# Turned tiles in the idle accumulator's bank, attention sums in the scores' bank, masks added by TensorE, and one granule kept whole in PSUM

## The chip, the cores and the metric

The kernel runs on one core of one Trainium2 chip. The metric is the device time of one execution in microseconds (us); a time of a kernel is the median of several runs. The profile shows one execution.

## The reference

The input x has 2048 rows of 1024 numbers. Its rows are normalised (layer norm) to xn, and the output is

    out = x + A(xn) + B(xn)

A is a recurrent attention over segments of 32 rows. Eight memory rows are carried from segment to segment:

```
mask[i, k] = (i < 8) or (i >= k)              # 40 x 40, row i asks, row k answers
for s in range(64):
    h = concat(mem, xn[32 s : 32 s + 32])     # 40 rows
    q, k, v = h Wq, h Wk, h Wv                # 32 heads of 128
    p = softmax(where(mask, q k^T / sqrt(128), -1e9))
    o = (p v) Wo                              # 40 rows of 1024
    mem = o[0:8];  out_A[segment s] = o[8:40]
```

B picks the two rows of xn with the highest router score and adds a gated MLP of them (1024 to 3584 and back). It runs at the end and is not touched by the change.

## The kernel before, in words

**Tiles.** A segment has 24 new rows that are computed at once with the eight memory rows (32 rows, `XM` = 24 and the memory), and eight left-over rows (`XL` = 8) that nothing later in the recurrence needs. The left-over rows of four segments are put together into one tile of 32 rows and go through the same weights in "left passes", spread by hand over the four segments of a group (`PASSES`, `COPIES`; j = s mod 4 is the place of a segment in its group). The matmuls have 32 columns of stationary data, so four of them stand side by side in the array (`tile_position`).

**Weights.** The weights are cut into 64 granules of 128 x 2048 bf16 (512 KB): 0 to 47 are Wq, Wk and Wv in six phases of eight (`PHASES`: q0, k0, q1, k1, v0, v1, the digit is the half of the heads), 48 to 63 are Wo. 44 granules stay in SBUF. Twenty (`STREAMED`) are read anew in every segment through a ring of five slots (`wstream`, tile `g`), in order, on SP's queue: whenever a streamed granule has been used (`release`, `after`), `fetch` issues the next of the list. From segment 1 on they come from a copy in DRAM (`wsc`), which segment 0 writes.

**Granules kept in PSUM.** Granule 6 (`KEPT_WHOLE`) lies whole in two PSUM banks and is copied back to SBUF in every segment (`bring_back`), with no transfer. The right half of granule 25 (`KEPT_PART`) lies in a third bank. Its left half (256 KB) is still streamed, and `kept_piece` copies two quarters of 512 columns into its slot on VectorE (hooks (2, 1) and (2, 2)). `keep` writes the kept pieces into PSUM in segment 0, by two transposes.

**PSUM.** There are eight banks of 2 KB per partition: two accumulators (`psA`, tiles PSm, WO), one for left passes (`psL`, PSl and WL), one for scores (`psS`, tile BS), one for turned tiles (`psT`, tile BT, with its parts `PTB`, `PTB2` and `OPB`), three for kept granules (`psK`). BS also holds the rows' means and deviations (`MR`, `ML`).

**One segment.** Phase p runs eight granules into PSm; ScalarE casts it to XB (L793) or VM (L803). Small work is hung on places (p, kc), that is behind granule 8 p + kc, by `hook`; TensorE runs it there in program order. At (p + 1, 3) `transposes` turns XB into BT (L624) and copies it out as QT (L632) or KT (L639). `turn_lx` and `new_qkl` do so for the left-over rows' q and k. `scores` at (2, 6) and (4, 6) writes the products into BS (L647, L649); VectorE then adds the masks there in three instructions (L656, L658), takes the maximum (L661) and subtracts it (L662). `exponent` (ScalarE, L666) and `soften` (VectorE, L671 to L682, the last read of BS is L679) follow at (3, 4) and (5, 0). `attend(half, ph)` multiplies by V (L696, L698) for two of the four column groups, and copies the sums to OT and OTL (L705, L707). It runs at (5, 4) and (5, 6) for half 0, with its sums in WO's bank and in BT, and inside the loop over Wo's granules at w = 5 and w = 8 for half 1, with its sums in BS and BT. With the last one the next segment's rows are turned into BT (`turn_rows`, L293). Wo's products go to WO (`project`, L574); VectorE adds them to x (L842), the memory rows are turned into the next segment's ST (`mem_to_st`), and the next segment starts.

**Order.** Each engine runs its instructions in the order of the program (`manual_schedule`); waits between engines are placed automatically from what each tile's bank holds.

Of the kernel before, what the change touches and what calls it, by code (L numbers as in the profile page):

```python
# [20 lines left out]
KEPT_PART = 25  # L21
# [29 lines left out]
def kernel(  # L51
# [69 lines left out]
    psT = ctx.enter_context(tc.tile_pool(name="psT", bufs=1, space=PSUM))  # L121
# [12 lines left out]
    wsc = {g: dram.tile([P, columns(g, 1).stop - columns(g, 1).start], BF16, name=f"wsc{g}")  # L134
           for g in streamed if g != KEPT_WHOLE}
# [19 lines left out]
    NEGR = CT[:, 13:14]  # L155
# [5 lines left out]
    BT = psT.tile([P, 512], F32, name="BT")  # L161
    SPS = BS[:, 0:8 * NK].rearrange("p (i a k) -> p i a k", i=4, a=2)
    PTB = BT[:, 0:256].bitcast(BF16)
    PTB2 = BT[:, 256:512].bitcast(BF16)
    OPB = BT[:, 256:256 + 4 * NK]
# [58 lines left out]
    def spread(t0, t1):  # L224
# [3 lines left out]
        PD = OPB  # L228
# [22 lines left out]
    def router_out():  # L251
        nc.vector.tensor_copy(out=RB, in_=RF)
        nc.tensor.transpose(out=PTB[0:NT, 0:P], in_=RB, identity=IDENT[:, :])
        RT = home(hx, [NT, P], BF16, "RT")
        nc.vector.tensor_copy(out=RT[:, :], in_=PTB[0:NT, 0:P])
        nc.gpsimd.dma_start(out=r_d[0].rearrange("(t p) -> t p", p=P), in_=RT[:, :])
# [33 lines left out]
    def turn(src, at=0):  # L290
        PTx = PTB[:, 256 * at:256 * (at + 1)].rearrange("p (c g r) -> p c g r", c=2, g=4)
# [12 lines left out]
    def new_st(turned):  # L304
        PTx, PTl = turned
# [23 lines left out]
    def sum_left(t, G):  # L329
# [31 lines left out]
    def keep(g, t):  # L361
        for c, K in KEPT_COLS[g].items():
            turned = PTB.rearrange("p (i r) -> p i r", i=4)
            for i in range(4):
                nc.tensor.transpose(out=turned[:, i, :], in_=t[:, 512 * c + P * i:512 * c + P * (i + 1)],
                                    identity=IDENT[:, :])
            XK = one.tile([P, 512], BF16, tag="vl0", name="XK")
            nc.vector.tensor_copy(out=XK[:, :], in_=PTB)
# [118 lines left out]
    def turn_lx():  # L487
        PTq = PTB2.rearrange("p (i c) -> p i c", i=4)
# [3 lines left out]
    def new_qkl():  # L492
        t = qkl[0] = one.tile([P, 4, 4, 4, XL], BF16, tag="bC", name="QKL")
        nc.scalar.copy(out=t.rearrange("p i m q r -> p (i m q r)"), in_=PTB2)

    def turn_first(mat, half, XBl):
        if mat == 0 and half == 0:
            qkl[0] = one.tile([P, 4, 4, 4, XL], BF16, tag="bC", name="QKL")
        PTq = PTB.rearrange("p (i c) -> p i c", i=4)
        for il in range(4):  # L500
            nc.tensor.transpose(out=PTq[:, il, :], in_=XBl[:, il * P:(il + 1) * P], identity=IDENT[:, :])
        nc.scalar.copy(out=qkl[0][:, :, 2 * half + mat, :, :],  # L502
                       in_=PTB.rearrange("p (i q s r) -> p i q s r", i=4, q=4, s=4)[:, :, :, 0, :])
# [103 lines left out]
    for s in range(NSEG):  # L607
# [7 lines left out]
        QT, KT, PTs, OT, nxt, sums = {}, {}, {}, {}, {}, {}  # L615
# [5 lines left out]
        def transposes(mat, half, XB):  # L621
            PTq = PTB.rearrange("p (i j r) -> p i j r", i=4, j=4)
# [3 lines left out]
            pv = PTq.rearrange("p i j r -> p (i j) r")  # L626
            with_left = s > 0 and mat == 0 and half == 0
# [13 lines left out]
        def scores(half):  # L641
            QKL = qkl[0]
            q, k = QT[half], KT[half]
            for il in range(4):
                for jq in range(4):
                    hh = 4 * il + jq
                    nc.tensor.matmul(SPS[32 * jq:32 * jq + 32, il, 0, :], lhsT=q[:, hh, :], rhs=k[:, hh, :],  # L647
                                     start=(il == 0), stop=True, tile_position=(0, 32 * jq), skip_group_check=True)
# [3 lines left out]
            for S4, m in ((SPS[:, :, 0, 0:XM], MASK), (SPS[:, :, 0, SEG:NK], None),  # L652
                          (SPS[:, :, 1, SEG:NK], MASK[:, 0:XL])):
                if m is not None:
                    m = m.unsqueeze(1).to_broadcast([P, 4, S4.shape[2]])
                    nc.vector.tensor_tensor(out=S4, in0=S4, in1=m, op=ALU.add)  # L656
                else:
                    nc.vector.tensor_scalar(out=S4, in0=S4, scalar1=NEGR, scalar2=None, op0=ALU.add)  # L658
# [26 lines left out]
        def attend(half, ph, turn_too=None):  # L685
            if half not in OT:
# [3 lines left out]
                sums[half] = [BS[:, 0:4 * NK] if half else nxt["wo"][:, 256:256 + 4 * NK], OPB]  # L690
            PTm, PTl = PTs[half]
            for il in range(4):
                for jl in range(2):
                    q0 = 32 * (2 * ph + jl)
                    o = sums[half][jl][:, il * NK:(il + 1) * NK]
# [6 lines left out]
            for jl in range(2):  # L702
                ov = sums[half][jl].rearrange("p (i q) -> p i q", i=4)
                copy = nc.scalar.copy if half == 0 or jl == 0 else nc.vector.tensor_copy
                copy(out=OT[half][:, 2 * ph + jl, :, :], in_=ov[:, :, 0:SEG])  # L705
                h0 = 16 * half + 8 * ph + 4 * jl
                copy(out=left_out()[:, h0:h0 + 4, j, :], in_=ov[:, :, SEG:NK])  # L707


# [53 lines left out]
        hook(5, 4, lambda: attend(0, 0))  # L763
        hook(5, 6, lambda: attend(0, 1))

        for p, (mat, half) in enumerate(PHASES):
# [24 lines left out]
            if mat < 2:  # L791
                XB = one.tile([P, 512], BF16, tag=("bE", "kt")[mat], name="XB")
                nc.scalar.copy(out=XB[:, :], in_=PSm[:, :])  # L793
                hooks.setdefault((p + 1, 3), []).insert(0, lambda m=mat, h=half, b=XB: transposes(m, h, b))
# [6 lines left out]
            else:  # L801
                VM[half] = one.tile([P, 512], BF16, tag=("bC", "bA")[half], name="VM")
                nc.scalar.copy(out=VM[half][:, :], in_=PSm[:, :])  # L803
                while stores:
# [7 lines left out]
        if s + 1 < NSEG:  # L812
            xn = norm_seg(s + 1)
            left_too = nxt["xl"] if j == 0 and G + 1 < NT else None
            turned = []
# [154 lines left out]
```

## Time and profile before

| | |
|---|---|
| time, median of 3 runs | 1903.38 us (1899.34 to 1905.05) |
| the profiled execution | 1896.06 us, span 1894.4 us |
| mean granted TensorE clock | 0.96 of full speed |
| TensorE matmul busy | 1572.3 us, 83% |
| VectorE, ScalarE, GpSimd busy | 875.6, 683.5, 441.5 us |
| moved by DMA | 712.41 MB, mean 376 GB/s |
| segment 0 done | at about 130 us; segments 1 to 63 until 1838 us, then B |

The profiled execution is somewhat quicker than the median of the runs; sums made in the profile are held against its own time. A row of the order of time reads: start, duration, engine, line, operation, tile written <- tiles read, shapes, count, and in brackets the idle time before it with what ended it. Rows of matmuls carry a modelled end, so rows that follow each other overlap. `g` is a slot of the ring, `wres` a resident granule.

### The profile page before, as it was taken

The page shows a single profiled execution, that of the slowest core. Times are in us where ns is not written, and L with a number is a line of the kernel's source. Part 1 is how long each engine was busy: PE and PEld are TensorE (multiplying, and loading weights), DVE is VectorE, ACT ScalarE, POOL GpSimd, SP SyncE. Part 2 cuts the span into 40 slices and gives each one's busy share as a digit, 9 for nine tenths or more (in the row PEclk, how much of TensorE's full clock was granted, in tenths as well). Part 3 has the DMA queues.
Part 4 walks back from the last instruction along what each step waited for, and adds up shares of the span by engine and source line. Part 5 has one row for each costly group of instructions (what it writes and reads, how often), then busy time and mean ns, then how long its engine had stood idle before and what let it go on. Part 6 is the DMA issues. An engine that isn't in the chain of part 4 may idle for free.

```text
span 1894.4 us, 82425 instructions
## 1 busy us (share of the span) xinstructions
PE 1572.3 (83%) x36000; PEld 880.0 (46%) x36000; DVE 875.6 (46%) x2865; ACT 683.5 (36%) x1916; POOL 441.5 (23%) x882
## 2 busy tenths in 40 slices
PE   3458888889888888898888988888888889888864
PEld 1124545455454444445454545445444554545443
DVE  6734544445444444544454444444444454444430
ACT  1123433344333433434333334333433343433320
POOL 3111313213131322213121322213132221312120
PEclk8669999999999999999999999999999999999985
DMA  9999999999999999999999999999999999999998
GB/s 370 398 368 379 369 386 373 391 378 390 393 360 375 368 380 372 379 372 374 401 365 374 370 388 370 355 383 374 379 364 387 377 392 378 364 395 362 374 388 331
DMA packets 232121, 712.41 MB, mean 376 GB/s; under 512 B 39296, under 2 KB 53168, under 8 KB 231760
## 3 DMA queue, kind: packets, MB, share of 16 engines
q1 hardware_dynamic: 194384, 671.18, 92.9%
q0 software_dynamic: 28736, 28.09, 4.6%
q10 hardware_dynamic: 8640, 7.87, 1.2%
q8 instruction: 282, 4.62, 0.9%
q14 instruction: 79, 0.65, 0.1%
HBM read 694.32 MB, written 22.29 MB: 378 GB/s over the span
## 4 chain that ended last, share of the span: by engine, by line
DMA 53%; PE 38%; DVE 5%; issue 2%; ACT 1%; SPq 1%; ACTq 0%; DVEq 0%
DMA g<-wsc 47%; PE PSm L774 21%; PE WO L574 4%; PE PSl L567 4%; PE BT L624 3%; PE WL L574 2%; DMA XP<-in_A_x_dram 2%; DMA MW<-in_B_w_gate_dram 1%; DVE XR L248 1%; DMA MW<-in_B_w_up_dram 1%; DMA g<-in_A_Wq_dram 1%; DMA wres<-in_A_Wo_dram 1%; PE BS L647 1%; DMA g<-in_A_Wo_dram 1%; PE BT L293 1%
## 5 line engine op out<-in xcount | busy, mean ns | idle before, releaser
L774 PE MATMUL PSm<-wres,ST 128*32 128x512 bf16 x8448 | 706.5, 383 | 9.1 <-DMA wres<-in_A_Wv_dram 3.5
L774 PEld LDWEIGHTS <-ST 128*32 128x32 bf16 x12288 | 328.6, 96 | 403.5 <-issue 176.3
L774 PE MATMUL PSm<-g,ST 128*32 128x512 bf16 x3588 | 361.9, 387 | 106.2 <-DMA g<-wsc 81.5
L574 PEld LDWEIGHTS <-OT 128*32 128x32 bf16 x8192 | 219.2, 97 | 153.3 <-issue 135.8
L793 ACT CAST XB<-PSm 128x512 bf16<-128x512 f32 x256 | 150.1, 586 | 310.8 <-PE PSm L774 309.9
L574 PE MATMUL WO<-wres,OT 128*32 128x256 bf16 x5632 | 238.3, 278 | 13.7 <-DMA wres<-in_A_Wo_dram 7.9
L483 POOL DMA_DIRECT2D LX<-ql_d x63 | 33.6, 533 | 825.9 <-PE WO L574 396.5
L574 PE MATMUL WO<-g,OT 128*32 128x256 bf16 x2560 | 132.3, 281 | 83.6 <-DMA g<-wsc 74.1
L567 PE MATMUL PSl<-wres,STL 128*32 128x512 bf16 x2112 | 192.7, 391 | 0.0
L844 POOL DMA_DIRECT2D out_dram<-X x256 | 129.4, 512 | 217.1 <-DVE X L842 168.3
L639 DVE COPY KT<-BT 128x512 bf16<-128x512 bf16 x112 | 45.7, 408 | 283.3 <-ACT XB L793 119.0
L273 POOL DMA_DIRECT2D X<-in_A_x_dram x256 | 129.7, 510 | 186.4 <-PE PSm L774 83.8
L377 ACT COPY BK<-KEPT 128x512 bf16<-128x512 bf16 x126 | 74.4, 590 | 129.3 <-PE WO L574 98.3
L632 ACT COPY QT<-BT 128x512 bf16<-128x512 bf16 x128 | 74.9, 585 | 122.2 <-PE BT L490 70.3
L567 PEld LDWEIGHTS <-STL 128*32 128x32 bf16 x3072 | 83.6, 98 | 54.0 <-issue 8.4
L624 PEld LDWEIGHTS <-XB 128*128 128x128 bf16 x1024 | 58.5, 98 | 107.6 <-ACT XB L793 66.4
L842 DVE TENSOR_TENSOR X<-WO,X 128x256 bf16<-128x256 f32 x64 | 27.2, 424 | 170.9 <-PE WO L574 170.9
L803 ACT CAST VM<-PSm 128x512 bf16<-128x512 f32 x128 | 75.6, 591 | 81.2 <-PE PSm L774 79.6
L696 PEld LDWEIGHTS <-VM 32*128 32x128 bf16 x2048 | 66.1, 91 | 82.9 <-issue 69.9
L624 PE MATMUL BT<-IDENT,XB 128*128 128x128 bf16 x1024 | 102.0, 222 | 1.4 <-ACT QKL L502 1.4
L381 DVE COPY g<-KEPT 128x512 bf16<-128x512 bf16 x126 | 47.6, 419 | 118.2 <-PE PSm L774 74.4
L705 DVE CAST OT<-BT 128x128 bf16<-128x128 f32 x128 | 37.3, 291 | 129.8 <-PE BT L293 68.8
(168 smaller groups left out, 2378.9 us busy)
## 6 DMA issues: line engine op xcount, KB each, us to landing
g<-wsc SPq DMA_DIRECT2D x1134, 512.0 KB, 6.1
g<-wsc SPq DMA_DIRECT2D x63, 256.0 KB, 5.4
LX<-ql_d POOLq DMA_DIRECT2D x63, 128.0 KB, 5.9
ql_d<-XBl ACTq DMA_DIRECT2D x60, 128.0 KB, 5.6
MW<-in_B_w_gate_dram SPq DMA_DIRECT2D x16, 448.0 KB, 9.1
MW<-in_B_w_up_dram SPq DMA_DIRECT2D x16, 448.0 KB, 9.1
wres<-in_A_Wk_dram SPq DMA_DIRECT2D x12, 512.0 KB, 11.5
MW<-in_B_w_down_dram SPq DMA_DIRECT2D x12, 512.0 KB, 10.1
```

Of the source, the lines that this page charges most:

```text
L273: nc.gpsimd.dma_start(out=X[s % 2][32 * g:32 * g + XM, :], in_=x2[s * SEG:s * SEG + XM, 256 * g:256 * (g + 1)])
L377: copy(out=back[c][:, :], in_=KEPT_COLS[KEPT_WHOLE][c])
L381: copy(out=t[:, 512 * c:512 * (c + 1)], in_=KEPT_COLS[g][c])
L567: nc.tensor.matmul(PSl[32 * jq:32 * jq + 32, :], lhsT=STL[:, g % KC, :], rhs=part(Gv, jq), start=first_, stop=last_, tile_position=(0, 32 ...
L574: nc.tensor.matmul(PS[32 * g:32 * g + 32, 0:256], lhsT=lhs(h), rhs=Gv[:, D * hs + 256 * g:D * hs + 256 * (g + 1)], start=(first and hs == ...
L624: nc.tensor.transpose(out=PTq[:, il, :, :].rearrange("p j r -> p (j r)"), in_=XB[:, il * P:(il + 1) * P], identity=IDENT[:, :])
L632: nc.scalar.copy(out=QT[half][:, :, :], in_=pv)
L696: nc.tensor.matmul(o, lhsT=VM[half][q0:q0 + 32, il * P:(il + 1) * P], rhs=PTm[q0:q0 + 32, il, 0:NK], start=True, stop=False, tile_position ...
L774: nc.tensor.matmul(PSm[32 * jq:32 * jq + 32, :], lhsT=ST[:, kc, :], rhs=part(Gv, jq), start=(kc == 0), stop=(kc == KC - 1), tile_position= ...
L793: nc.scalar.copy(out=XB[:, :], in_=PSm[:, :])
L803: nc.scalar.copy(out=VM[half][:, :], in_=PSm[:, :])
L844: nc.gpsimd.dma_start(out=out2[s * SEG:s * SEG + XM, 256 * g:256 * (g + 1)], in_=OB[32 * g:32 * g + XM, :])
```

## The change

Tile BT and its bank go. What lay there lies elsewhere:

- Turned tiles (`turned(n)`, half n of 256 fp32 columns) lie in the accumulator that is idle: `idle[0]` is the last PSm that has been cast out. The next phase but one writes into this bank again.
- The attention sums of half 0 lie in WO's bank (as before) and in BS; those of half 1 in the idle accumulator and in BS. The hooks of `attend(0, ...)` move from (5, 4) and (5, 6) to (5, 5) and (5, 7).
- The masks are no longer added by VectorE behind the scores. TensorE writes them into BS before the scores, in three matmuls with the identity, behind the transposes of k at (2, 3) and (4, 3); the scores accumulate on them. The row constant `NEGR` becomes bf16.
- The freed bank is a fourth one for kept granules: granule 25 (`KEPT_SLOT`) is kept whole. From segment 1 on nothing of it is loaded and nothing of it is written to `wsc`. It still takes its turn in the ring's slots, and four copies fill the slot: the first on ScalarE at (1, 7), three on VectorE at (2, 0), (2, 1) and (2, 2).
- `norm_left` moves from (5, 3) to (4, 4) in segments after the first.

```diff
-KEPT_PART = 25
+KEPT_SLOT = 25
...
-        if s > 0 and g == KEPT_WHOLE:
+        if s > 0 and g in (KEPT_WHOLE, KEPT_SLOT):
             return None
-        return slice(0, 1024 if s > 0 and g == KEPT_PART else 2048)
+        return slice(0, 2048)
...
-    BT = psT.tile([P, 512], F32, name="BT")
+    idle = [psA.tile([P, 512], F32, tag="acc", name="START")]
+
+    def turned(n=0):
+        return idle[0][:, 256 * n:256 * (n + 1)].bitcast(BF16)
...
-    KEPT = [psK.tile([P, 1024], BF16, name=f"KEPT{b}") for b in range(3)]
-    KEPT_COLS = {KEPT_WHOLE: {0: KEPT[0][:, 0:512], 1: KEPT[0][:, 512:1024], 2: KEPT[1][:, 0:512], 3: KEPT[1][:, 512:1024]},
-                 KEPT_PART: {2: KEPT[2][:, 0:512], 3: KEPT[2][:, 512:1024]}}
+    KEPT = [psK.tile([P, 1024], BF16, name=f"KEPT{b}") for b in range(4)]
+    KEPT_COLS = {g: {c: KEPT[2 * n + c // 2][:, 512 * (c % 2):512 * (c % 2 + 1)] for c in range(4)}
+                 for n, g in enumerate((KEPT_WHOLE, KEPT_SLOT))}
...
         def transposes(mat, half, XB):
-            PTq = PTB.rearrange("p (i j r) -> p i j r", i=4, j=4)
+            PTq = turned().rearrange("p (i j r) -> p i j r", i=4, j=4)
...
+            if mat == 1:
+                for S4, m in ((SPS[:, :, 0, 0:XM], MASK), (SPS[:, :, 0, SEG:NK], NEGR.to_broadcast([P, XL])),
+                              (SPS[:, :, 1, SEG:NK], MASK[:, 0:XL])):
+                    nc.tensor.matmul(S4, lhsT=IDENT[:, :], rhs=m.unsqueeze(1).to_broadcast([P, 4, S4.shape[2]]),
+                                     start=(m is MASK), stop=False, skip_group_check=True)
...
                     nc.tensor.matmul(SPS[32 * jq:32 * jq + 32, il, 0, :], lhsT=q[:, hh, :], rhs=k[:, hh, :],
-                                     start=(il == 0), stop=True, tile_position=(0, 32 * jq), skip_group_check=True)
+                                     start=False, stop=True, tile_position=(0, 32 * jq), skip_group_check=True)
...
-            for S4, m in ((SPS[:, :, 0, 0:XM], MASK), (SPS[:, :, 0, SEG:NK], None),
-                          (SPS[:, :, 1, SEG:NK], MASK[:, 0:XL])):
-                if m is not None:
-                    m = m.unsqueeze(1).to_broadcast([P, 4, S4.shape[2]])
-                    nc.vector.tensor_tensor(out=S4, in0=S4, in1=m, op=ALU.add)
-                else:
-                    nc.vector.tensor_scalar(out=S4, in0=S4, scalar1=NEGR, scalar2=None, op0=ALU.add)
...
-        def attend(half, ph, turn_too=None):
+        def attend(half, quads, turn_too=None):
...
-                sums[half] = [BS[:, 0:4 * NK] if half else nxt["wo"][:, 256:256 + 4 * NK], OPB]
+            banks = [(idle[0] if half else nxt["wo"])[:, 256:256 + 4 * NK], BS[:, 0:4 * NK]]
...
-            hook(2, 1, lambda: kept_piece(KEPT_PART, 2, nc.vector.tensor_copy))
-            hook(2, 2, lambda: kept_piece(KEPT_PART, 3, nc.vector.tensor_copy))
+            for c in range(4):
+                hook(1 + (c + 7) // 8, (c + 7) % 8, lambda c=c: kept_piece(KEPT_SLOT, c, (nc.scalar.copy if c == 0 else
+                                                                                         nc.vector.tensor_copy)))
...
-            hook(5, 3, lambda: norm_left(nxt["xl"], G + 1))
+            hook(*((4, 4) if s > 0 else (5, 7)), lambda: norm_left(nxt["xl"], G + 1))
...
-        hook(5, 4, lambda: attend(0, 0))
-        hook(5, 6, lambda: attend(0, 1))
+        hook(5, 5, lambda: attend(0, [0, 1]))
+        hook(5, 7, lambda: attend(0, [2, 3]))
...
                 nc.scalar.copy(out=XB[:, :], in_=PSm[:, :])
+                idle[0] = PSm
```

In the other places PTB and PTB2 become `turned()` and `turned(1)`, and OPB becomes `idle[0]`.

More of the change, by code (lines that the diff above doesn't have):

```diff
@@ L252, in router_out @@
         nc.vector.tensor_copy(out=RB, in_=RF)
-        nc.tensor.transpose(out=PTB[0:NT, 0:P], in_=RB, identity=IDENT[:, :])
+        PTR = turned()[0:NT, 0:P]
+        nc.tensor.transpose(out=PTR, in_=RB, identity=IDENT[:, :])
         RT = home(hx, [NT, P], BF16, "RT")
-        nc.vector.tensor_copy(out=RT[:, :], in_=PTB[0:NT, 0:P])
+        nc.vector.tensor_copy(out=RT[:, :], in_=PTR)
         nc.gpsimd.dma_start(out=r_d[0].rearrange("(t p) -> t p", p=P), in_=RT[:, :])
@@ L493, in new_qkl @@
         t = qkl[0] = one.tile([P, 4, 4, 4, XL], BF16, tag="bC", name="QKL")
-        nc.scalar.copy(out=t.rearrange("p i m q r -> p (i m q r)"), in_=PTB2)
+        nc.scalar.copy(out=t.rearrange("p i m q r -> p (i m q r)"), in_=turned(1))
     def turn_first(mat, half, XBl):
@@ L701, in attend @@
                 turn_too()
[L702 to L706, printed above, removed]
+            for n, (quad, sum_) in enumerate(sums.items()):
+                ov = sum_.rearrange("p (i q) -> p i q", i=4)
+                copy = nc.vector.tensor_copy if n and half else nc.scalar.copy
+                copy(out=OT[half][:, quad, :, :], in_=ov[:, :, 0:SEG])
+                h0 = 16 * half + 4 * quad
                 copy(out=left_out()[:, h0:h0 + 4, j, :], in_=ov[:, :, SEG:NK])
@@ L803 @@
                 nc.scalar.copy(out=VM[half][:, :], in_=PSm[:, :])
+                idle[0] = PSm
                 while stores:
@@ L877 @@
                                 op0=ALU.subtract, op1=ALU.mult)
-    PXS = PTB[:, 0:2 * KC].rearrange("p (k c) -> p k c", c=2)
+    idle[0] = psA.tile([P, 512], F32, tag="acc", name="PXS")
+    PXS = turned()[:, 0:2 * KC].rearrange("p (k c) -> p k c", c=2)
     for kc in range(KC):
```

47 lines of the change are left out of this document (22 added, 25 removed).

## The prediction

> **What bounds the kernel now.** I read the profile page first: the busy shares, the DMA slices, the queues and the chain.
>
> ```profile
> span 1894.4 us, 82425 instructions
> PE 1572.3 (83%) x36000; PEld 880.0 (46%) x36000; DVE 875.6 (46%) x2865; ACT 683.5 (36%) x1916; POOL 441.5 (23%) x882
> ...
> DMA  9999999999999999999999999999999999999998
> ...
> q1 hardware_dynamic: 194384, 671.18, 92.9%
> ...
> DMA 53%; PE 38%; DVE 5%; issue 2%; ACT 1%; SPq 1%; ACTq 0%; DVEq 0%
> ```
>
> TensorE is the busiest engine by the first row, but the DMA row stands at 9 in all slices but the last, and more than half of the ending chain is DMA. So the question is whether TensorE has slack left. Next I asked for the windows: all segments from the second on, then one segment with j = s mod 4 = 2 and the j = 3 segment behind it (columns: length, busy time and count per engine, granted clock, DMA share, GB/s).
>
> ```profile
> 129.40:1837.75 1708.35, 1496.93 (x34690) 838.23 (x34690) 791.99 (x2646) 661.91 (x1866) 406.38 (x805) 0.99 1.00 376
> 1348.91:1375.25 26.34, 22.86 (x525) 12.26 (x520) 12.12 (x40) 10.33 (x29) 4.70 (x10) 1.00 0.99 379
> 1375.25:1403.06 27.81, 25.55 (x601) 14.20 (x597) 12.22 (x40) 11.30 (x31) 6.93 (x14) 1.00 1.00 369
> ```
>
> The DMA share is 1.00 over 63 segments, which take 1708.35 / 63 = 27.1 us each. Then TensorE's order of time in the j = 2 segment and the waits of the whole span.
>
> ```profile
> 1364.69 0.40 PE L774 MATMUL PSm<-g,ST 128*32 128x512 bf16 x4 [0.47 <-DMA g<-wsc]
> 1364.90 0.62 PE L774 MATMUL PSm<-wres,ST 128*32 128x512 bf16 x8
> 1365.91 0.40 PE L774 MATMUL PSm<-g,ST 128*32 128x512 bf16 x4 [0.39 <-DMA g<-wsc]
> ...
> 1374.58 0.40 PE L574 MATMUL WO<-g,OT 128*32 128x256 bf16 x8 [0.41 <-DMA g<-wsc]
> ```
>
> ```profile
> PE PSm L774 <- DMA g<-wsc: 81.5, 173, 1.7
> PE WO L574 <- DMA g<-wsc: 74.1, 161, 1.9
> DVE OT L705 <- PE BT L293: 68.8, 63, 2.7
> PE WO L696 <- ACT OTL L707: 11.5, 15, 2.1
> ```
>
> The rows with `g` are streamed granules 39, 42 and, last, 62. From 39 to 62 there are eight steps in 9.89 us: 1.24 us for each granule of 512 KB. In the second half of a segment TensorE runs at the pace at which granules land. It waited 81.5 + 74.1 = 155.6 us in 334 waits, 2.5 us a segment. More is hidden: a granule's row lasts 0.40 us, yet the next starts 0.21 us behind it (1364.69, 1364.90), and a wait is counted only from the modelled end; 334 times 0.19 us adds 1.0 us a segment. So TensorE's path without these waits is about 27.1 - 3.5 = 23.6 us against 27.1 us of transfers, and the DMA is the bound.
>
> **The change part by part.**
>
> *The transfer removed.* Granule 25's second load goes.
>
> ```profile
> g<-wsc SPq DMA_DIRECT2D x1134, 512.0 KB, 6.1
> g<-wsc SPq DMA_DIRECT2D x63, 256.0 KB, 5.4
> ```
>
> 63 loads of 256 KB leave SP's queue. At 1.24 us for 512 KB one is worth 0.62 us; at the queue's mean (92.9% of 1894.4 us is 1760 us for 671.18 MB, so 0.262 MB take 0.69 us) a little more. Upper end: 63 x 0.69 = 43 us. Segment 0 also no longer writes these 256 KB out, about 1 us.
>
> *Copies instead.* All four quarters of granule 25 now come out of PSUM, two more than before: one on ScalarE at phase 1, one on VectorE at phase 2.
>
> ```profile
> L377 ACT COPY BK<-KEPT 128x512 bf16<-128x512 bf16 x126 | 74.4, 590 | 129.3 <-PE WO L574 98.3 <-issue 31.0
> L381 DVE COPY g<-KEPT 128x512 bf16<-128x512 bf16 x126 | 47.6, 419 | 118.2 <-PE PSm L774 74.4 <-DMA g<-wsc 27.9 <-PE PSl L567 15.9
> L656 DVE TENSOR_TENSOR BS<-BS,CT 128x96 f32<-128x96 f32 (+1 forms) x256 | 59.6, 233 | 80.5 <-PE BS L649 76.0
> L658 DVE TENSOR_SCALAR BS<-BS,CT 128x32 f32<-128x32 f32 x128 | 33.1, 259 | 4.5
> ```
>
> They cost 0.59 and 0.42 us on engines that are 36% and 46% busy, and wait only for a slot freed in phase 0. The DVE copies stand idle before (118.2 us in all), so no one is late: zero, or about 0.3 us on TensorE where the ScalarE copy pushes the next XB. VectorE loses the masks: (59.6 + 33.1) / 63 = 1.5 us a segment.
>
> *Masks on TensorE.* Three identity matmuls per half, six a segment, behind the four transposes.
>
> ```profile
> 1362.42 0.40 PE L624 MATMUL BT<-IDENT,XB 128*128 128x128 bf16 x4
> 1362.75 0.40 PE L774 MATMUL PSm<-g,ST 128*32 128x512 bf16 x4
> ...
> L370 PE MATMUL KEPT<-IDENT,XK 128*128 128x128 bf16 x24 | 3.2, 279 | 11.6 <-DVE XK L368 11.6
> ```
>
> Four identity matmuls of 128 columns take 0.33 us from start to the next start, 0.08 each; the dearest identity group has 0.28. No such masks are in the trace, so 0.08 and 0.28 are the ends; they are nearest to the transposes beside which they stand, and I take 0.09: 0.55 us a segment (ends 0.5 and 1.7). A gain is excluded here, as TensorE had none of this work.
>
> *Attention sums in the scores' bank.* `attend(0, ...)` now writes BS and so must wait until `soften(1)` has read it (L679); before, it could run ahead. Behind it on TensorE stand granules 46, 47 and all of Wo.
>
> ```profile
> 1364.34 0.27 DVE L656 TENSOR_TENSOR BS<-BS,CT 128x96 f32<-128x96 f32 x1 [0.56 <-PE BS L649]
> ...
> 1365.16 0.49 DVE L661 TENSOR_REDUCE NM<-BS 128x8 f32<-128x320 f32 x1
> ...
> 1367.78 0.21 DVE L679 TENSOR_TENSOR OTL<-BS,DN 128x64 bf16<-128x64 f32 x1
> ```
>
> Today BS is free at 1367.99, 3.65 us after the first mask. Without masks the reduce takes the first mask's place, 0.82 us earlier, so 2.83 us remain, and about 3.1 us from the scores' last matmul. TensorE by itself needs seven granules, 7 x 0.215 = 1.5 us, to reach the new hook (5, 5): it would stand 1.4 us in j = 0 and 2. In j = 1 three passes for the left-over rows before that hook (0.65 us) fill half of this, in j = 3 six fill nearly all. Mean 0.9 us (ends 0 and 1.5).
>
> *Banks shared.* The waits row `DVE OT L705 <- PE BT L293` shows that copies out of one part of a bank are ordered behind writes to another part. So Wo's first matmuls wait until ScalarE has copied the sums that lie in WO's bank:
>
> ```profile
> 905.78 0.19 ACT L707 CAST OTL<-WO 128x32 bf16<-128x32 f32 x1
> ```
>
> ```profile
> 905.63 0.40 PE L774 MATMUL PSm<-g,ST 128*32 128x512 bf16 x4
> 906.02 0.62 PE L574 MATMUL WO<-wres,OT 128*32 128x256 bf16 x16
> ```
>
> The copy ends at 905.97, Wo starts at 906.02, 0.39 us behind a granule that lasts 0.215. With the second attend moved behind granule 47 that cover is gone: 0.3 us more. Likewise PSm of phase p + 2 waits for the copies out of the turned tile:
>
> ```profile
> 893.42 0.82 PE L774 MATMUL PSm<-wres,ST 128*32 128x512 bf16 x12
> ```
>
> ```profile
> 893.57 0.59 ACT L494 COPY QKL<-BT 128x512 bf16<-128x512 bf16 x1
> ```
>
> The x12 are granules 14, 15 and 16, so phase 2 begins at 893.85, the copy ends at 894.16: 0.3 us of wait, 0.25 on the mean, since passes fill it in j = 2. In phases 3 to 5 the copies end first.
>
> *Sum.* TensorE gets 0.55 + 0.9 + 0.3 + 0.25 = 2.0 us a segment, 25.6 us in all, and the transfers 27.1 - 0.65 = 26.5 us. The transfers stay the bound by 0.9 us on the mean; with the high ends (1.7 + 1.5 + 0.3 + 0.3 = 3.8) TensorE would, by 0.9.
>
> j = 3 is tighter: in its last third TensorE hardly waits for the DMA. There one wait goes:
>
> ```profile
> 1395.33 0.18 ACT L707 CAST OTL<-WO 128x32 bf16<-128x32 f32 x1 [1.46 <-DVE PT L682]
> ```
>
> `attend(0, 1)` waits 0.8 us there for this copy (the row `PE WO L696 <- ACT OTL L707`: 11.5 us in 15 waits), which hangs on `soften(1)`, 0.82 us earlier without masks. That pays for the masks and Wo's wait; I keep 0.2 us of gain there. Elsewhere I keep 0.6 of 0.65, as the margin varies: 47 x 0.6 + 16 x 0.2 = 31 us, of which I take off 1 us for granule 25's two more pieces in segment 0, where four more transposes and a copy for each lie beside loads. The profiled execution took 1896.06 us (span 1894.4), so 1866; the median of the runs is 1903.38, 7 us above it, so 1873.
>
> **The rivals.**
>
> *TensorE takes half of it back* (0.17). The wait for BS is 1.5 us in every segment, and phase 4 also waits 0.3: 2.9 us on TensorE, level with the transfers at 26.5. Where two limits are level each wins at times; I put it at 12 us of gain, 1891. For it: in j = 0 and 2 there are no passes in phase 5. Against: five slots let TensorE be two granules late, 2.5 us, at no cost.
>
> *The masks make TensorE the bound* (0.14, slower). The mask matmuls write four separate runs of 24 or 8 columns, which no matmul of the trace does. Should each last as long as a 512-column matmul from start to modelled end, 0.40, six cost 2.4 us instead of 0.55, the path is 27.5 us, 0.4 above today's 27.1, and 63 x 0.4 = 25 us are lost: 1928. It decides from 0.34 us a matmul (2.05 us for six). Against: the rows of identity matmuls with contiguous output, 0.08 in step. The Trainium skill, "PSUM — Partial Sum Buffer", Specifications (TRN2), says that any non-contiguous access pattern slows matmuls significantly and gives no figure; no run here shows it yet, and by that rule the time is this rival's.
>
> *Nothing is gained* (0.09). Granule 25's slot carries no transfer from phase 0 to phase 3, so at most four loads are in flight, not five; were the rate set by their number, the queue would lose what it saves: 1903, give or take 4. For it: a load lands 6.1 us after issue, about the time of five. Against: the DMA share is 1.00, so the engines have work throughout, and 256 KB less landed only 0.7 us sooner.
>
> **How the numbers follow.** Forecast 0.60: 1873, its own range 1860 (all 43 us) to 1886. The range 1858 to 1897 takes in the second case and part of the fourth and leaves out the slower one. About 0.3%, 5.7 us, is what a measurement can tell from no change. Faster: 0.60 and nearly all of the second, 0.76; same: most of the fourth, 0.08; slower: the third and the rest of the fourth, 0.16.
>
> **What would show it.** Right: no 256 KB loads from wsc; DMA share 1.00 again; segments of about 26.6 us; the waits of TensorE for `g<-wsc` down from 155.6 us to near 60; new waits of `attend` for VectorE's L679 and of Wo for ScalarE; six mask matmuls in about 0.09 us steps. Wrong: a DMA share under 0.98 in j = 0 to 2, waits for DMA almost gone with segments of 27 us (TensorE the bound), or a granule pitch above 1.3 us in phase 5.

## The result: slower by 1.1%

The changed kernel takes 1922.83 us (median of four runs, 1921.66 to 1924.08) against 1901.74 us (1899.34 to 1905.05): 1.011 times as long, 95% interval 1.009 to 1.0129. Some 31 us were forecast to go; 21 us came.

The page of the profile after, the rows that answer to those of before:

```profile
span 1920.1 us, 82800 instructions
PE 1595.6 (83%) x36400; PEld 913.4 (48%) x36400; DVE 809.5 (42%) x2546; ACT 702.2 (37%) x1979; POOL 442.1 (23%) x881
...
DMA  9999999999999999999999999999999999999998
...
q1 hardware_dynamic: 185312, 654.66, 90.8%
...
DMA 45%; PE 43%; DVE 5%; ACT 4%; issue 3%; SPq 0%; ACTq 0%; POOL 0%; DVEq 0%
...
g<-wsc SPq DMA_DIRECT2D x1134, 512.0 KB, 6.0
```

The 256 KB loads are gone and 16.5 MB less is moved by q1. The slices of the DMA row still stand at 9. A load takes 6.0 us instead of 6.1. The window over the same 63 segments (length, busy time and count by engine, granted clock, DMA share, GB/s):

```profile
129.21:1862.63 1733.42, 1517.32 (x35068) 868.78 (x35068) 726.69 (x2330) 680.89 (x1929) 407.16 (x805) 0.98 0.98 361
```

A segment takes 1733.42 / 63 = 27.51 us, against 27.12. The loss of 0.40 us a segment lies in the recurrence and not in segment 0 or B. The rate fell from 376 to 361 GB/s: fewer bytes were moved, and the time did not fall. TensorE's waits after:

```profile
PE PSm L775 <- DMA g<-wsc: 93.7, 173, 1.7
...
PE WO L576 <- ACT OTL L709: 34.8, 64, 0.9
PE WO L576 <- DMA g<-wsc: 27.4, 61, 1.8
...
PE PSm L775 <- ACT QKL L496: 7.4, 37, 0.2
PE BS L698 <- DVE BX L679: 4.8, 10, 0.9
PE BS L698 <- DVE OTL L679: 3.0, 7, 0.8
```

The waits for loads fell from 155.6 to 121.1 us, those of Wo for loads from 74.1 to 27.4, while those of PSm rose from 81.5 to 93.7. New waits stand in front of Wo: 34.8 us for the copy of the left-over rows' sums out of WO's bank, in 64 waits, one in each segment.

### The profile page after: what moved, and what is told of

Read it like the earlier page. It is cut to its first block, busy times and chain, and to the rows that moved or that the text cites. A ratio compares the mean times of both kernels' runs of the same rounds, so it can differ in the third digit from the quotient of the medians.

```text
span 1920.1 us, 82800 instructions
## 1 busy us (share of the span) xinstructions
PE 1595.6 (83%) x36400; PEld 913.4 (48%) x36400; DVE 809.5 (42%) x2546; ACT 702.2 (37%) x1979; POOL 442.1 (23%) x881
## 4 chain that ended last, share of the span: by engine, by line
DMA 45%; PE 43%; DVE 5%; ACT 4%; issue 3%; SPq 0%; ACTq 0%; POOL 0%; DVEq 0%
DMA g<-wsc 37%; PE PSm L775 20%; PE WO L576 8%; PE PSl L569 4%; PE PSm L626 3%; DMA XP<-in_A_x_dram 2%; PE WL L576 1%; DMA MW<-in_B_w_gate_dram 1%; DMA MW<-in_B_w_up_dram 1%; ACT QKL L496 1%; DVE XR L249 1%; DVE DN L671 1%; ACT VL L593 1%; PE PSm L698 1%; DMA g<-in_A_Wq_dram 1%
## 5 line engine op out<-in xcount | busy, mean ns | idle before, releaser
L775 PE MATMUL PSm<-wres,ST 128*32 128x512 bf16 x8448 | 713.8, 383 | 17.2 <-ACT QKL L496 7.4
L775 PE MATMUL PSm<-g,ST 128*32 128x512 bf16 x3588 | 361.3, 385 | 109.4 <-DMA g<-wsc 93.7
L576 PE MATMUL WO<-wres,OT 128*32 128x256 bf16 x5632 | 246.8, 287 | 45.6 <-ACT OTL L709 34.8
L383 DVE COPY g<-KEPT 128x512 bf16<-128x512 bf16 x189 | 68.5, 418 | 382.4 <-ACT g L383 336.9
L576 PE MATMUL WO<-g,OT 128*32 128x256 bf16 x2560 | 137.1, 287 | 36.0 <-DMA g<-wsc 27.4
L639 ACT COPY QT<-PSm 128x512 bf16<-128x512 bf16 x128 | 74.9, 585 | 130.9 <-PE PSm L492 77.7
L671 DVE TENSOR_REDUCE DN<-BS 128x8 f32<-128x320 f32 x128 | 62.9, 491 | 133.1 <-ACT BS L666 133.1
L698 PE MATMUL BS<-PT,VM 32*128 32x40 bf16 x1024 | 87.7, 178 | 20.3 <-DVE RI L270 9.4
L626 PE MATMUL PSm<-IDENT,XB 128*128 128x128 bf16 x1024 | 102.0, 222 | 1.6 <-ACT QKL L504 1.4
L661 DVE TENSOR_REDUCE NM<-BS 128x8 f32<-128x320 f32 x128 | 62.8, 491 | 77.1 <-PE BS L656 77.1
```

The lines of the kernel that those rows point to most:

```text
L576: nc.tensor.matmul(PS[32 * g:32 * g + 32, 0:256], lhsT=lhs(h), rhs=Gv[:, D * hs + 256 * g:D * hs + 256 * (g + 1)], start=(first and hs == ...
L626: nc.tensor.transpose(out=PTq[:, il, :, :].rearrange("p j r -> p (j r)"), in_=XB[:, il * P:(il + 1) * P], identity=IDENT[:, :])
L639: nc.scalar.copy(out=QT[half][:, :, :], in_=pv)
L671: nc.vector.tensor_reduce(out=DN[:, :], in_=S8, axis=AX.X, op=ALU.add)
L698: nc.tensor.matmul(o, lhsT=VM[half][q0:q0 + 32, il * P:(il + 1) * P], rhs=PTm[q0:q0 + 32, il, 0:NK], start=True, stop=False, tile_position ...
L775: nc.tensor.matmul(PSm[32 * jq:32 * jq + 32, :], lhsT=ST[:, kc, :], rhs=part(Gv, jq), start=(kc == 0), stop=(kc == KC - 1), tile_position= ...
```

## The experiments

Ratios are to the kernel before, run on the same chip, with 95% intervals.

### Structure and transfer apart

**e1_structure_only**: the changed kernel with granule 25 as before (right half kept, left half loaded, two copies).

```diff
-        return slice(0, 2048)
+        return slice(0, 1024 if s > 0 and g == KEPT_SLOT else 2048)
```

> The changed kernel, but granule 25 is loaded by half as before (256 KB a segment come back; the freed bank stays empty). Theory P (pace): from granule 9 to 36 TensorE sets the pace, so the transfer saved there buys nothing, and what the change adds on TensorE costs the 20 us. Then loading the half again costs next to nothing: 1923, 1917 to 1930. Theory S (dead slot): the slot that granule 25 holds without a transfer keeps the queue from running ahead, which itself costs; with the half loaded again it costs as little as before: 1910 to 1917. Theory T (my forecast's prices): the transfer is worth 40 us and the moves cost 60: 1950 to 1965.

Measured: 1915.24 us, 1.0073 (1.0037 to 1.0108). It lies in the range of theory S, though the interval reaches into that of P.

**e2_no_transfer**: the kernel before, with no load of granule 25 and four copies into its slot.

```diff
+            for c in range(4):
+                hook(1 + (c + 7) // 8, (c + 7) % 8, lambda c=c: kept_piece(KEPT_PART, c, (nc.scalar.copy if c == 0 else nc.vector.tensor_copy)))
```

> The kernel before, but nothing of granule 25 is loaded from segment 1 on: its slot is still taken in turn and filled by four copies out of PSUM, at the changed kernel's places (its left half gets the right half's numbers, so this part of the computation is changed). Nothing else moves. P: 1896 to 1903, as the transfer buys nothing there. S: 1900 to 1912, the dead slot costs what the transfer saves, or more. T: 1858 to 1870.

Measured: 1909.69 us, 1.0033 (1.0005 to 1.0061), again in the range of S. So the saved load with its copies is no gain but a small loss by itself, and 0.73% + 0.33% is about the 1.1% of the whole change: the two parts add up.

**e3_out_of_ring**: the kernel before, granule 25 takes no slot; the resident granule 24 is read for it, without copies.

```diff
-                Gv = back if s > 0 and g == KEPT_WHOLE else granule(g)
+                Gv = back if s > 0 and g == KEPT_WHOLE else granule(24 if s > 0 and g == KEPT_PART else g)
```

> The kernel before, but granule 25 is out of the ring from segment 1 on: no transfer, no slot, no copies (the phase reads granule 24 twice, so this part of the computation is changed). P: 1893 to 1903, no better than with the dead slot but for the copies. S: 1858 to 1872, since all five slots carry transfers. T: 1858 to 1870, the same as with the dead slot.

Measured: 1888.3 us, 0.9903 (0.9858 to 0.9948). No range takes it in: P began at 1893, S and T ended at 1872 and 1870.

**e8_dead_slot_one_copy**: as e2, but one copy alone into the slot; three quarters are read from granule 24.

```diff
+                if s > 0 and g == KEPT_PART:
+                    Gv = [res_tiles[24][:, 512 * c:512 * (c + 1)] for c in range(3)] + [Gv[:, 1536:2048]]
```

> The kernel before with granule 25's slot taken and not loaded, as e2, but only one quarter copied out of PSUM; the other three quarters are read from resident granule 24 (this part of the computation is changed). If the dead slot is what parts e2 from e3: 1903 to 1911, as e2. If the four copies are: 1884 to 1892, as e3.

Measured: 1899.67 us, 0.9982 (0.9958 to 1.0006), between the two ranges. Taken one after the other: with load, slot and two copies gone it is -1.0% (e3). With the slot held again and one copy into it, +0.8% (e8 against e3, the intervals lie apart). With three copies more, +0.5% (e2 against e8, the intervals just meet at their ends). While the slot is held, the load and one copy less are worth 0.2% (e8), with an interval that reaches to no gain at all. The forecast had -2.3% at most for the load, none for the slot and about none for the copies.

### The parts of the structure

**e4_attend_back**, **e5_masks_back** and **e6_turned_back** are e1 with one of its parts as before: the attention sums in a bank of their own with the old hooks, the masks on VectorE, the turned tiles in a bank of their own.

```diff
e4: -        hook(5, 5, lambda: attend(0, [0, 1]))
    +        hook(5, 4, lambda: attend(0, [0, 1]))
e5: +                    nc.vector.tensor_tensor(out=S4, in0=S4, in1=m, op=ALU.add)
e6: -        return idle[0][:, 256 * n:256 * (n + 1)].bitcast(BF16)
    +        return BT[:, 256 * n:256 * (n + 1)].bitcast(BF16)
```

> As e1_structure_only (granule 25 loaded by half), and the attention sums lie again in BS, WO and a bank of their own, with attend at (5, 4) and (5, 6). Left of the change: turned tiles in the idle accumulator and masks on TensorE. If the waits of attend for soften and of Wo for ScalarE cost the most (P as I priced it, 1.2 of 2.0 us a segment): 1905 to 1912. If masks and the turned tiles cost it: 1917 to 1923. If attend's waits are hidden by the DMA: as e1.

> As e1_structure_only (+14 us to the kernel before), with the masks added by VectorE again. If the masks' six matmuls are what costs TensorE most: 1900 to 1908, beside 1902 before. If shortening soften's chain matters more to attend, which now waits for it, than the matmuls cost: 1918 to 1935, since BS comes free 0.82 us later in each half. If the two cancel: 1912 to 1918.

> As e1_structure_only, with the turned tiles in a bank of their own again (attention sums and masks stay as changed). If the wait of a phase for the copies out of the idle accumulator (0.25 us a segment by my sum) is all on the path: 1898 to 1904. If it is hidden by the DMA: 1912 to 1919, as e1.

Measured: 1913.42 us, 1.0048 (1.0024 to 1.0073); 1956.49 us, 1.0279 (1.0237 to 1.0322); 1907.04 us, 1.0018 (0.9992 to 1.0043). Against e1's 1.0073 the turned tiles in the accumulator cost about 0.55% and the attention sums in BS about 0.25%. Both intervals overlap e1's, so these two sizes are only indicated; e4 and e6 lie between their ranges. That the masks belong on TensorE, once `attend` waits for `soften`, is clear: on VectorE they cost 2% more, above the dearest range that had been named. `attend`'s waits for `soften` (`PE BS <- DVE OTL` and `BX`) are 35.5 us there, against 4.5 in e1.

### The saved load elsewhere

**e7_fetch_past_dead_slot** (the changed kernel, the next load issued at once when granule 25 takes its slot), **e11_copies_on_vector** (its first copy on VectorE) and **e12_keep_45** (granule 45 kept in place of 25, copied at phase 4).

```diff
e7:  +        if s > 0 and c is None:
     +            fetch()
e11: -                hook(1 + (c + 7) // 8, (c + 7) % 8, lambda c=c: kept_piece(KEPT_SLOT, c, (nc.scalar.copy if c == 0 else nc.vector.tensor_copy)))
     +                hook(1 + (c + 7) // 8, (c + 7) % 8, lambda c=c: kept_piece(KEPT_SLOT, c, (nc.vector.tensor_copy)))
e12: -KEPT_SLOT = 25
     +KEPT_SLOT = 45
```

> The whole changed kernel, but when granule 25 takes its slot without a transfer the next granule is fetched at once too, and none when granule 25 is released: four live loads run ahead again instead of three. S (the dead slot keeps the queue from running ahead): the 25 us between e2 and e3 come back, 1893 to 1906. P (TensorE's pace in that stretch alone): no change, 1917 to 1927.

> The whole changed kernel, with the first of granule 25's four copies moved from ScalarE to VectorE, same place. If the ScalarE copy, which stands ahead of the cast of the next XB, is what e2 lost beside e8: 1908 to 1916. If the copies only cost because there are more of them on VectorE, or nothing: 1920 to 1928.

> The whole changed kernel, but it keeps granule 45 (phase 5) in PSUM instead of 25, which is loaded whole again; three copies on ScalarE and one on VectorE in phase 4. The bytes are the changed kernel's, the place of the transfer saved is the stretch in which TensorE waits for transfers. Place: 1885 to 1908, quicker than the changed kernel by 15 us or more. Load, or TensorE's own chain: 1917 to 1930.

Measured: 1922.2 us, 1.0094 (1.0057 to 1.0131); 1922.73 us, 1.0096 (1.0063 to 1.013); 1934.18 us, 1.0167 (1.014 to 1.0194). None helps. The ScalarE copy is not what it hangs on (e11). For e7, theory S had expected 1893 to 1906, which did not come. But the edit moves only the place of the issue in the program: the ring still has five slots, and the load that is issued early still waits until its slot is freed. So e7 says nothing about the slot. e12 lies above both of its ranges and 11 us above the changed kernel: a whole transfer saved where TensorE waits for transfers, with its slot held and its copies in phase 4, gains nothing either.

**e9_half_of_42_dropped** and **e10_half_of_29_dropped**: the kernel before with the right half of one more granule not loaded, and read from a resident one.

```diff
-        return slice(0, 1024 if s > 0 and g == KEPT_PART else 2048)
+        return slice(0, 1024 if s > 0 and g in (KEPT_PART, 42) else 2048)
```

> The kernel before, with the second half of granule 42 (phase 5) neither stored to wsc nor loaded from segment 1 on: its slot takes the other 256 KB, and the last two quarters are read from resident granule 41 (this part of the computation is changed). No dead slot, no copies, nothing else moved. Place (TensorE waits for transfers in phase 5 and Wo, so a byte saved there counts): 1866 to 1884. Load (a byte saved counts anywhere, as I forecast): 1861 to 1875, as e10. If no byte counts, since other chains bound the segment: 1897 to 1905.

> The same with granule 29 (phase 3, where TensorE sets the pace; the last two quarters are read from resident granule 30, so this part of the computation is changed). Place: 1893 to 1903. Load: 1861 to 1875.

Measured: 1893.92 us, 0.996 (0.9938 to 0.9983); 1899.66 us, 0.9993 (0.9971 to 1.0016). Here nothing is added: no copy, no slot without a load, no bank shared. 256 KB less a segment, worth 39 to 43 us by the forecast, buys 8 us (3 to 12 by the interval) and 1 us (-3 to 6). e10 lies in the range for Place. e9 lies in none, nearest to the one in which no byte counts. So a saved byte hardly buys time, neither where TensorE waits for transfers nor where it doesn't; that it buys more at 42 than at 29 is only indicated, as the intervals overlap.

### The paths without transfers

**e13_no_stream_before**, **e14_no_stream_after**: no streamed granule is loaded after segment 0. **e15_fewer_loads_before**, **e16_fewer_loads_after**: eight of the nineteen are not.

```diff
+UNLOADED = [9, 17, 29, 36, 42, 47, 53, 59]
...
+        if s > 0 and g in UNLOADED:
+            return res_tiles[min(r for r in resident if r > g)]
```

> The kernel before, with no streamed granule loaded after segment 0: wherever a streamed granule was used, the next resident granule is read (granule 25's kept quarters and their copies go too). TensorE has the same instructions, with no load to wait for. Forecast's theory (TensorE's path without waits for loads is 23.6 us a segment): 1903 - 63 x 3.5 = 1682 us, 1650 to 1710. Rival (the path, with the casts, copies out and sums that feed it, stands just below 27.1 us, and a saved load meets it at once): 1820 to 1880, and the waits of TensorE are then for VectorE and ScalarE.

> The changed kernel with no streamed granule loaded after segment 0, read from the next resident granules in the same way (no copies of granule 25). Against e13 it gives what the masks, the attention sums and the turned tiles add to the path where no load hides it. The forecast priced +2.0 us a segment: e13 + 126 us. If the structure costs only what e1_structure_only showed: e13 + 14 us. If the masks on TensorE save more than the rest costs (e5_masks_back was 41 us slower than e1): e13 or below.

> The kernel before, with eight more granules (9, 17, 29, 36, 42, 47, 53, 59) not loaded after segment 0 and the next resident granule read for them; granule 25 as before. 4 MB less a segment of 10.6. By the forecast's theory the path of 23.6 us rules: about 1682 us, as e13. By the rival: within 20 us of e13, wherever that is. If the loads' number in flight or their fixed latency rules and not bytes: 1800 or more with e13 far below.

> The changed kernel with the same eight granules not loaded after segment 0. Whatever is left between e16 and e15 is path and not transfers: forecast's price 2.0 us a segment, +126 us; by e1_structure_only and e2_no_transfer +14 to +20 us.

Measured: 1679.4 us, 0.8841 (0.8793 to 0.8888); 1747.4 us, 0.9203 (0.9148 to 0.9257); 1690.87 us, 0.8902 (0.8854 to 0.8951); 1753.96 us, 0.9223 (0.9171 to 0.9274). The windows of e13 and then of e14:

```profile
128.63:1629.46 1500.83, 1433.88 (x34690) 827.37 (x34690) 740.53 (x2519) 655.69 (x1866) 404.90 (x805) 1.00 0.09 27
```

```profile
129.10:1695.94 1566.84, 1448.73 (x35068) 856.37 (x35068) 657.58 (x2141) 651.69 (x1866) 405.24 (x805) 1.00 0.09 26
```

TensorE's path is 1500.83 / 63 = 23.8 us a segment before and 24.9 us after, at 0.09 of DMA share. The rival that I had put up after the first results, that other chains stand just below 27.1 us, falls: it gave 1820 to 1880 us. The changed path is 1.05 us longer, and that is still 2.2 us below the 27.1 us of a segment before. Transfers hold both kernels. In time e14 is 68 us above e13 and e16 63 us above e15, where the forecast's price gave 126 and e1 14. The window of e15 and its loads:

```profile
129.00:1637.28 1508.28, 1437.11 (x34690) 829.74 (x34690) 782.32 (x2645) 656.17 (x1866) 406.41 (x805) 1.00 0.79 253
```

```profile
g<-wsc SPq DMA_DIRECT2D x630, 512.0 KB, 4.5
g<-wsc SPq DMA_DIRECT2D x63, 256.0 KB, 4.2
```

With eight loads fewer a segment takes 1508.28 / 63 = 23.94 us, nearly the path alone. A load of 512 KB lands in 4.5 us when (10 x 4.5 + 4.2) / 23.94 = 2.1 loads are in flight on the mean, and in 6.1 us when (18 x 6.1 + 5.4) / 27.12 = 4.25 are. Twice the loads in flight land in 1.36 times the time, so a part of the time to landing doesn't grow with their number. e15 can't tell bytes from loads in flight: it lies where the forecast's theory put it, at about 1682, and not at the 1800 or more that had been expected if the loads in flight ruled. But eleven loads of 4.5 us over five slots are 10 us, and at 1.24 us each they are 14 us, both far below the path.

### Six slots

That leaves the number of slots to be tried by itself. SP's own waits, of before and then of after, point at it: the queue that issues the loads stands waiting for a slot. The rows with `g<-wsc` are the first half of such a wait, for the slot's last load to land; the rows with PE are the second, for TensorE to have used it.

```profile
SPq L354 <- PE PSm L774: 452.5, 648, 3.8
SPq L354 <- DMA g<-wsc: 384.5, 722, 2.2
SPq L354 <- PE PSl L567: 220.9, 224, 3.0
SPq L354 <- PE WO L574: 131.9, 252, 1.6
SPq L354 <- PE WL L574: 45.7, 58, 1.9
```

```profile
SPq L356 <- PE PSm L775: 457.4, 568, 4.2
SPq L356 <- DMA g<-wsc: 364.7, 512, 3.6
SPq L356 <- PE PSl L569: 185.9, 192, 3.0
SPq L356 <- PE WO L576: 180.6, 253, 2.4
SPq L356 <- PE WL L576: 67.0, 59, 2.1
SPq L356 <- PE BS L700: 53.0, 54, 1.7
```

**e17_six_slots_before** and **e18_six_slots_after**: the ring has six slots. The resident granule 15 makes room, and 16 is read in its place.

```diff
-N_SLOT = 5
+N_SLOT = 6
...
+        if g == DROPPED:
+            g = NEXT
```

> The kernel before with a ring of six slots instead of five. The room comes from resident granule 15, which is not kept: granule 16 is read in its place. Loads, bytes and matmuls stay the same. If bytes set the time of the transfers: no change, within 0.3% of before. If the five slots do: clearly faster; five slots hold 18 loads and a half of 6.1 us each in 27.1 us (4.2 in flight), six would hold 5.2; if a load took no longer the segment would fall by a sixth to below TensorE's own path of 23.6 us, so 1720 to 1850 us, and the waits of TensorE for g<-wsc shrink to less than half of 155.6 us.

> The changed kernel with six slots in the same way. If bytes set the time: at most the slot without a load is given back, 1900 to 1915 us. If slots do: far below 1900 and nearer to its own floor of 1747 us (e14) than before's twin is to 1679 (e13), since it has fewer loads: the two six-slot kernels would stand within 1% of each other or the changed one slower by what its path costs more.

Measured: 1825.14 us, 0.96 (0.9561 to 0.9638); 1852.27 us, 0.9724 (0.9693 to 0.9756). The window, the loads and the waits of e17:

```profile
127.78:1760.94 1633.16, 1482.12 (x34690) 835.61 (x34690) 789.38 (x2646) 656.91 (x1866) 407.58 (x805) 1.00 1.02 394
```

```profile
g<-wsc SPq DMA_DIRECT2D x1134, 512.0 KB, 6.7
g<-wsc SPq DMA_DIRECT2D x63, 256.0 KB, 6.0
```

```profile
PE WO L579 <- DMA g<-wsc: 17.7, 45, 1.3
PE PSm L779 <- DMA g<-wsc: 17.5, 48, 1.1
```

The same loads, the same bytes and the same matmul counts take 76 us less. The waits for loads go from 155.6 to 35.2 us, and 394 GB/s are moved where 376 stood at a DMA share of 1.00. So it is the number of slots that cost these 76 us. Where it did, the same segment of both kernels shows. The windows run from granule 13 to 36 and from 39 to 62, first of before, then of e17:

```profile
1354.92:1362.75 7.83, 7.83 (x164) 3.76 (x156) 3.57 (x11) 4.45 (x9) 2.02 (x4) 1.00 0.94 323
1364.69:1374.58 9.89, 7.86 (x214) 5.17 (x214) 5.61 (x21) 4.33 (x17) 0.53 (x1) 1.00 1.02 411
```

```profile
1298.82:1306.65 7.83, 7.83 (x164) 3.76 (x157) 3.58 (x11) 4.45 (x9) 2.01 (x4) 1.00 1.04 404
1307.95:1318.16 10.21, 7.79 (x242) 5.21 (x224) 5.83 (x22) 4.16 (x17) 0.53 (x1) 1.00 1.03 418
```

In the first stretch TensorE is busy throughout and takes 7.83 us in both. With five slots 323 GB/s are moved meanwhile, with six 404. Granules 25 and 29 land on the mean 1.2 us before TensorE uses them in the kernel before, and so long they hold their slots; 39 to 50 land 0.04 to 0.30 us before. In the second stretch, where TensorE waits for granules, 411 and 418 GB/s are moved, much the same. No 10 us in a row move more than 417 GB/s before or 420 in e17. So the sixth slot lets loads run ahead while TensorE sets the pace; how fast they land where TensorE waits, it doesn't change. In this one segment the second stretch is no shorter; on the mean of 62 segments it takes 10.11 us with six slots and 10.99 with five, since fewer of its loads come late.

The changed kernel with six slots is 71 us quicker than with five and still 27 us slower than its twin: from phase 0 to phase 3 it has one slot less for loads, and its path is longer.

## Why the prediction was wrong, point by point

**The step that failed** is the price of the transfer: "At 1.24 us for 512 KB one is worth 0.62 us", and with it "the transfers 27.1 - 0.65 = 26.5 us", which takes a whole segment for time of the bytes. Measured, 256 KB less are worth 8 us at granule 42 and 1 us at 29 (e9, e10), and 3 us (0 to 8 by the interval) where the slot stays held (e8). 39 to 43 had been forecast.

The pitch of 1.24 us itself is sound where it was read. From 39 to 62 granules land one behind the other at the rate of the transfers. Two landings that follow each other are most often 1.2 to 1.3 us apart, with five slots (291 of 721 pairs that the trace has) as with six (346 of 749). But 18 granules and a half at 1.24 us are 22.9 us, and a segment takes 27.1. Even all bytes of a segment, those of the other queues too, would take 376 x 27.12 / 417 = 24.5 us at the highest rate above, by this estimate. The rest is time in which the queue doesn't run at this pace, as in the stretch with 323 GB/s. At 29 there is no wait for a load that a saved byte could shorten: in 62 segments TensorE has none at granules 25, 29 and 33. At 42 the load does come sooner: in segments at full clock TensorE reaches 42 and the granules up to 50 some 0.5 us earlier, counted from 39. At 53 only 0.26 us are left, and in the next segment's phase 4, at 36, 0.11 us, which is 7 us in all. For 53 the reason is in the order of the ring: its load is issued when 39 has been used, and 39 comes no sooner. Where the rest goes stays open. In e9 the stretch of the same segment reads

```profile
1364.77:1374.93 10.16, 7.71 (x214) 5.21 (x214) 5.20 (x19) 4.33 (x17) 0.53 (x1) 1.00 0.99 371
```

that is, fewer bytes at a lower rate, 371 GB/s instead of 411, and in this segment no less time (on the mean of 62 it is 10.76 us instead of 10.99).

**"The DMA share is 1.00, so the engines have work throughout"** was the argument against the third rival. e17 moves 394 GB/s at a share of 1.02 and before 376 at 1.00, and the stretch with 323 GB/s has 0.94, so a share near 1 is not a full queue. The Trainium skill, "Perfetto Trace Analysis", Identifying the Most-Contended Engine, says that occupancy misleads for DMA since there are 16 engines; the two windows agree. The Trainium skill, "DMA: Bandwidth & Descriptors", Anatomy of one DMA, gives a fixed 2.0 us and 436 GB/s for the software path. For 512 KB that is 3.2 us, an estimate for one load alone; no run here had one load alone, and these loads go by another queue. That a part of a load's time doesn't grow with its own bytes is what 6.1 against 5.4 us shows.

**The third rival** (a slot without a load leaves four in flight) was given 0.09 and came nearest to the mechanism. e3 and e8 put the slot, with one copy, at +0.8%, 15 us, and the loads in flight fell from 4.25 to 18 x 6.0 / 27.51 = 3.93. It gave 1903, since it counted nothing for the path: "The transfers stay the bound" hid the path's growth there, and the first rival's "five slots let TensorE be two granules late, 2.5 us, at no cost" leans on the same thought. But a ring whose slots come free when TensorE has used them passes a later use on to the next load.

**TensorE's path of 23.6 us** was right: 23.8 us in e13, and 1679.4 us against the 1682 that it gives.

**The path's growth**, priced at 2.0 us a segment, is 1.05 us (e14 against e13). By its terms: the masks took 0.36 us instead of 0.55; the row below is three of them in e14, and the next matmul starts 0.18 us behind the first.

```profile
908.56 0.40 PE L629 MATMUL PSm<-IDENT,XB 128*128 128x128 bf16 x4
908.79 0.25 PE L635 MATMUL BS<-CT,IDENT 128*128 128x96 bf16 x3
908.97 0.40 PE L775 MATMUL PSm<-wres,ST 128*32 128x512 bf16 x4
```

The three waits, in e14 where no load hides them:

```profile
PE WO L579 <- ACT OTL L712: 34.4, 64, 0.9
PE BS L701 <- DVE OTL L682: 33.1, 33, 1.3
PE BS L701 <- DVE BX L682: 19.5, 15, 1.3
...
PE PSm L775 <- ACT QKL L499: 11.8, 48, 0.4
```

`attend` waits (33.1 + 19.5) / 63 = 0.83 us for `soften` (0.9 forecast), Wo 0.55 us for ScalarE (0.3 forecast, the one that was too small), PSm 0.19 us for the turned tile (0.25). Against them goes a wait of e13, that of `attend` for ScalarE's copy, 0.52 us a segment, which e14 doesn't have; the forecast had counted it in j = 3 alone. The four terms are 1.93 us by these rows, near the 2.0 that were forecast, and 1.41 without the wait that goes; the last 0.36 us down to 1.05 are not traced.

```profile
PE WO L699 <- ACT OTL L710: 32.5, 48, 2.6
```

In the changed kernel as it runs, `attend`'s wait shows in 17 waits of 7.8 us in all only, since TensorE comes late to it anyway.

**The masks as a bound** (0.14) didn't come. The rule of the Trainium skill, "PSUM — Partial Sum Buffer", Specifications, that a non-contiguous access pattern slows matmuls significantly can't be tested by these rows. Three masks write 96 + 32 + 32 = 160 columns in 0.18 us, the four transposes beside them 512 contiguous ones in 0.23 us: the same 0.06 us a step, but 1.1 ns a column against 0.45. What the rows do show is that the 0.34 us a matmul that this rival needed isn't there.

**The copies** were priced at nothing or 0.3 us; three more cost about 0.5%, 0.15 us a segment (e2 against e8, only indicated). Which of their waits it is stays open; moving the ScalarE one to VectorE changed nothing (e11).

**The signs.** Of those named for "right" the missing 256 KB loads, the new waits and the mask steps came; the segments of 26.6 us did not, and TensorE's waits for loads went only a third of the way to 60. The share of 0.98 lies at the edge of what had been named as a sign that TensorE is the bound; e14 shows that it was not. The pitch, named as wrong above 1.3 us in phase 5, stayed: in the same segment after, 39 to 62 take 9.86 us, 1.23 us a granule. No sign had been named for a queue that is held up by its slots.

What is not settled: how the structure's 0.73% comes about while its path stands 2.2 us below the transfers. The traces say where: at full clock TensorE of the changed kernel reaches 47 earlier than before, by 0.30 us counted from 39, and 50 later by 0.26. Between them stand the second `attend` and Wo's wait. That later uses free slots later fits with this, with SP's new row for `BS` (53.0 us in 54 waits) and with e6, but no run isolates it.

## What to carry to other kernels

Before a transfer is priced by the pitch of a stretch, multiply the pitch by the number of loads and hold it against the time of the whole loop. Here 22.9 us stood against 27.1, and half a load less bought 1 to 8 us instead of some 40. Then ask, stretch by stretch, whether the consumer waits for loads, at which rate they move, and what the issuing queue waits for. The time to landing divided by the number of buffers doesn't settle it, since it gives the pitch whenever all buffers are in flight, whatever sets it. One buffer more at the same bytes does settle it. A kept piece that still takes a turn in the ring gives back most of what its load saved.

## What the runs showed of the hardware

A DMA share near 1 (0.98, 1.00 and 1.02) stood at 361, 376 and 394 GB/s. Over 10 us in a row the most that was moved is 417 GB/s before and after, and 420 in e17. A load of 512 KB took 4.5, 6.1 and 6.7 us with 2.1, 4.25 and (18 x 6.7 + 6.0) / 25.92 = 4.9 loads in flight. A straight line through these three points, an estimate that holds between them alone, has 3 us and 0.75 us for each load in flight.

The granted clock of single segments fell below 0.99 in 9 of 63 segments before and 13 after, against 2 in e13 and e17 and 20 in e18. Held against the mean of the same j at full clock, these segments cost 12.6 us before and 13.2 after, so the clock is no part of the difference of the two, but 9 us of e17's gain.
